# Loading V in 16 KB rows and reordering P by a permuting matmul and a DVE transpose, in a one-core decode kernel

## The chip, the cores and the metric

The kernel runs on one core of a Trainium2 chip. The metric is the device time of one execution in microseconds (us), lower is better. The kernel before takes 418.68 us (median of 4 runs, 418.47 to 418.81). PE is the matmul engine, PEld its weight loads, DVE the vector engine, ACT the scalar engine, POOL the GpSimd engine, and SP issues the DMAs.

## The reference

One token goes through an attention layer with a long cache, beside a small MLP. Cut to what matters here:

```python
# A_x [1,1,1024], k_cache and v_cache [1, 4, 65536, 128] bf16, wq [1024, 4096], wo [4096, 1024]
q = (xn @ wq) -> 32 heads of 128; 8 query heads share one of 4 cache heads
scores = einsum("bhqd,bhkd->bhqk", q, k) * 128 ** -0.5
p = softmax(scores); o = einsum("bhqk,bhkd->bhqd", p, v)
out = x + xn + ...  # o @ wo, and an MLP of w1, w2 [1024, 1024], w3 [1024, 3584], w4 [3584, 1024] on xn
```

K and V are 67.1 MB each, of about 170 MB in all. Each byte is read once and used for 8 query heads, so the kernel is mostly a matter of reading memory: its DMA queue fills 97.8% of the span of the 16 engines (page below).

## The kernel before

It works through 32 blocks (4 cache heads with 8 blocks of 8192 cached positions each). A block brings 2 MB of K and 2 MB of V. The parts that the change and the argument touch (cuts are marked with `# ...`):

```python
NK, NV = 3, 4          # buffers for K and V
KA, VA = 3, 3          # K and V are asked for three blocks ahead

def issue_k(n):        # partition p holds rows 64p..64p+63: one run of 16 KB
    # ...
    e.dma_start(out=Kn[:, s, :, :].rearrange("p c d -> p (c d)"),
                in_=kv_src(A_k_cache, n).rearrange("(p c) d -> p (c d)", p=P))
def issue_v(n):        # four groups of 16 rows a partition: four runs of 4 KB
    # ...
    e.dma_start(out=Vn[:, s, :, :, :].rearrange("p a t d -> p a (t d)"),
                in_=kv_src(A_v_cache, n).rearrange("(a i t) d -> i a (t d)", a=4, i=P))

def Ttr(n, idx):       # DVE: transposes a quarter of K in 32x32 squares, Kn -> X
    # ...
def EXP(n):            # ACT: p = exp(scale * S + running minimum), written at a stride of 8 bytes
    e.activation(p_sb[:, m, :].rearrange("p (cl p0 ch) -> p cl ch p0", cl=4, p0=32),
                 S_ps[:, :].rearrange("p (cl ch p0) -> p cl ch p0", cl=4, ch=4), ACTF.Exp, # ...
def PTr(n):            # PE: four 128x128 transposes of p
    for c2 in range(4): e.transpose(out=PT_ps[:, c2*P:(c2+1)*P], in_=p_sb[:, m, c2*P:(c2+1)*P], identity=ident_bf[:])
def PTevac(n):         # ACT: PSUM -> SBUF, reordered
    e.activation(pT_sb[:, m, :, :, :].rearrange("p r c g -> p c r g"), PT_ps[:, 0:512].rearrange(# ...
def PV(n):             # PE: 16 matmuls of 128x32 by 128x512
    # ...

for n in range(NBLK):
    issue_k(n + KA); issue_v(n + VA); run_pending(n, "dma")   # weights and output rows
    QK(n)
    Ttr(n + 1, [0])
    stats1(n); MB(n); stats2(n); EXP(n)
    Ttr(n + 1, [1, 2, 3])
    PTr(n); PTevac(n); PV(n); FLASH(n)
    # ...
# after the last block: combine the head, ten output rows (wo), seven chunks of w4, output
```

All DMAs are issued by SP in program order, on one queue (30304 of the 30330 packets on the page below). K of block n+3 waits until the transposes of block n have freed its buffer.

Of the kernel before, what the change touches and what calls it, by code (L numbers as in the profile page):

```python
# [6 lines left out]
BF = mybir.dt.bfloat16  # L7
# [124 lines left out]
def bass_parallel_sum__gqa_block_cached__mixer_s_mlp__decode_kernel(  # L132
# [11 lines left out]
    out: bass.AP,  # L144
    dbg=None,
):
    P = 128
# [17 lines left out]
    with ExitStack() as es:  # L165
# [3 lines left out]
        def sb(name, shape, dt):  # L169
            return E(nc.sbuf_tensor(name, shape, dt))  # L170
# [41 lines left out]
        X = sb("X", [P, 2, 8192], BF)  # L212
        Vn = sb("Vn", [P, NV, 4, 16, P], BF)
        tmpO = sb("tmpO", [P, 2, 513], F32)
        p_sb = sb("p_sb", [P, 2, 512], BF)
        pT_sb = sb("pT_sb", [P, 2, 16, 4, G], BF)
        mrow = sb("mrow", [P, 2], F32)
# [23 lines left out]
        S_ps = ps("S_ps", [P, 512], F32)  # L241
        PTB_ps = ps("PTB_ps", [P, 512], F32)
        PT_ps = PTB_ps[:, 0:256].bitcast(BF)
        MB_ps = PTB_ps[:, 256:272]
        OT_ps = ps("OT_ps", [P, 512], F32)
# [36 lines left out]
        def mk_slots():  # L282
            sl = {}
            sl["ws"] = [_Slot(WS[:, i, :], b_WS[i], _DmaChan(sem("d_ws%d" % i))) for i in range(NWS)]
            sl["x"] = [_Slot(X[:, i // 2, 4096 * (i % 2):4096 * (i % 2) + 4096], b_X[i // 2][2 * (i % 2):2 * (i % 2) + 2], _DmaChan(sem("d_x%d" % i)))
                       for i in range(4)]
            sl["k"] = [[_Slot(Kn[:, s, 32 * i:32 * i + 32, :].rearrange("p c k -> p (c k)"), [b_Kn[s][i]], _DmaChan(sem("d_kh%d_%d" % (s, i))))
                        for i in range(2)] for s in range(NK)]
            sl["v"] = [[_Slot(Vn[:, s, 2 * i:2 * i + 2, :, :].rearrange("p a t d -> p (a t d)"), [b_Vn[s][i]], _DmaChan(sem("d_vh%d_%d" % (s, i))))
                        for i in range(2)] for s in range(NV)]  # L290
            return sl
# [4 lines left out]
        for t_, val in ((ident_bf, 0.0), (ident_f, 0.0), (ones_f, 1.0), (sel16, 1.0), (selGT_bf, 1.0), (selTT, 1.0),  # L296
                        (neghalf, -0.5), (permWE, 1.0), (maskA, 1.0), (g_bf, 0.0)):
            evs.append(q_pool.op(lambda e, t_=t_, val=val: e.memset(t_[:], val)))
# [13 lines left out]
                                            compare_op=ALU.is_equal, fill=0.0, base=0, channel_multiplier=1))  # L312
        q_pool.op(lambda e: e.affine_select(out=permWE[:], in_=permWE[:], pattern=[[-64, 2], [-1, 2], [0, 4], [-2, 32]],
                                            compare_op=ALU.is_equal, fill=0.0, base=0, channel_multiplier=1))
        ev = q_pool.op(lambda e: e.affine_select(out=maskA[:], in_=maskA[:], pattern=[[-32, 4], [0, 8]],
# [109 lines left out]
        def issue_v(n):  # L425
            if n >= NBLK:
                return
            s = n % NV
            _dma(q_sp, ch_v[s], lambda e, s=s, n=n: e.dma_start(out=Vn[:, s, :, :, :].rearrange("p a t d -> p a (t d)"),  # L429
                                                                in_=kv_src(A_v_cache, n).rearrange("(a i t) d -> i a (t d)", a=4, i=P)),  # L430
                 writes=b_Vn[s])
# [20 lines left out]
        def QK(n):  # L452
            h = n // NB
            xs = n % 2
            fns = []
            for we in range(4):
                w_hi, e_ = divmod(we, 2)
                for c_mid in range(4):
                    mv = bass.AP(X[:].tensor, xs * 8192 + 4 * c_mid * 128 + w_hi * 64 + e_, [[xstep, P], [128, 4], [2048, 4], [2, 32]])
                    fns.append(lambda e, we=we, c_mid=c_mid, mv=mv, h=h: e.matmul(  # L460
                        S_ps[32 * c_mid:32 * c_mid + 32, :], Yall[:, h, we, :, :].rearrange("p a g -> p (a g)"), mv,
                        start=(we == 0), stop=(we == 3), tile_position=(0, 32 * c_mid)))
            _grp(q_pe, fns, reads=b_X[xs] + [b_Y], writes=[b_S])
# [7 lines left out]
        def MB(n):  # L471
            m = n % 2
            _op(q_pe, lambda e, m=m: e.matmul(MB_ps, Lmat[:, :], Rm[:, m, :], start=True, stop=True),  # L473
                reads=[b_R[m], b_const], writes=[b_MB, b_PT])

        def stats2(n):
            _op(q_dve, lambda e, n=n: e.tensor_reduce(out=Bst[:, n:n + 1], in_=MB_ps, axis=AX.X, op=ALU.min),  # L477
                reads=[b_MB, b_PT], writes=[b_Bcol[n]])

        def EXP(n):  # L480
# [5 lines left out]
            else:  # L486
                ko = (nb - 1) % 2
                _op(q_dve, lambda e, n=n, ko=ko, kn=kn: e.tensor_tensor(out=brun[:, kn:kn + 1], in0=brun[:, ko:ko + 1], in1=Bst[:, n:n + 1], op=ALU.min),  # L488
                    reads=[b_brun[ko], b_Bcol[n]], writes=[b_brun[kn]])
            _op(q_act, lambda e, n=n, m=m, kn=kn: e.activation(p_sb[:, m, :].rearrange("p (cl p0 ch) -> p cl ch p0", cl=4, p0=32),  # L490
                                                               S_ps[:, :].rearrange("p (cl ch p0) -> p cl ch p0", cl=4, ch=4),
                                                               ACTF.Exp, bias=brun[:, kn:kn + 1], scale=SCALE, accum_out=tmpO[:, m, 512:513]),
                reads=[b_S, b_brun[kn]], writes=[b_p[m], b_tmpO[m]])
            if nb > 0:
# [3 lines left out]
                _op(q_act, lambda e, m=m: e.activation(ff[:, m, 0:1], dd[:, m, 0:1], ACTF.Exp), reads=[b_dd[m]], writes=[b_ff[m]])  # L498

        def PTr(n):  # L500
            m = n % 2
            fns = []
            for c2 in range(4):
                fns.append(lambda e, c2=c2, m=m: e.transpose(out=PT_ps[:, c2 * P:(c2 + 1) * P], in_=p_sb[:, m, c2 * P:(c2 + 1) * P], identity=ident_bf[:]))  # L504
            _grp(q_pe, fns, reads=[b_p[m], b_const], writes=[b_PT, b_MB])

        def PTevac(n):
            m = n % 2
            _op(q_act, lambda e, m=m: e.activation(pT_sb[:, m, :, :, :].rearrange("p r c g -> p c r g"),  # L509
                                                   PT_ps[:, 0:512].rearrange("p (c r g) -> p c r g", c=4, r=16), ACTF.Copy),  # L510
                reads=[b_PT, b_MB], writes=[b_pT[m]])

        def PV(n):
            m = n % 2
            vs = n % NV
            fns = []
            for r in range(16):
                q4 = r % 4
                fns.append(lambda e, r=r, q4=q4, m=m, vs=vs: e.matmul(OT_ps[32 * q4:32 * q4 + 32, :], pT_sb[:, m, r, :, :].rearrange("p c g -> p (c g)"),  # L519
                                                                     Vn[:, vs, r % 4, 4 * (r // 4):4 * (r // 4) + 4, :].rearrange("p t d -> p (t d)"),  # L520
                                                                     start=(r < 4), stop=(r >= 12), tile_position=(0, 32 * q4)))
            _grp(q_pe, fns, reads=[b_pT[m]] + b_Vn[vs], writes=[b_OT])
# [166 lines left out]
        for n in range(NBLK):  # L689
# [10 lines left out]
            EXP(n)  # L700
            Ttr(n + 1, [1, 2, 3])
            run_pending(n, "b")
            PTr(n)
            PTevac(n)
            PV(n)
            FLASH(n)
# [19 lines left out]
        _op(q_dve, lambda e: e.tensor_copy(orow[:, :], M0_ps[0:KT_D, 300:300 + P]), reads=[b_M0], writes=[b_orow])  # L726
        if dbg:
            taps = dict(xn=xn[:, :], qT_bf=qT_bf[:, :], Bst=Bst[:, :], Lst=Lst[:, :], O_acc=O_acc[:, :], maskT=maskT[:, :, :].rearrange("p t g -> p (t g)"),
                        OTh_bf=OTh_bf[:, :, :].rearrange("p h g -> p (h g)"), acc=acc[:, :], fin=fin[:, :], p_sb=p_sb[:, :, :].rearrange("p m k -> p (m k)"),
                        pT_sb=pT_sb[:, :, :, :, :].rearrange("p m r c g -> p (m r c g)"), hsT=x1[:, :], h1g=h1g_bf[:, :], gh=gh_bf[:, :],  # L730
                        Yall=Yall[:, :, :, :, :].rearrange("p h w a g -> p (h w a g)"), X=X[:, 0, :], Lmat=Lmat[:, :], sel16=sel16[:, :], selG=selG_f[:, :])
            ch_dbg = _DmaChan(sem("d_dbg"))
            for qq in (q_pe, q_dve, q_act):
                q_pool.wait((qq.sem, qq.cnt))
            for name, dap in dbg.items():
                src = taps[name]
                _dma(q_pool, ch_dbg, lambda e, dap=dap, src=src: e.dma_start(out=dap, in_=src))
                q_pool.wait((ch_dbg.sem, 16 * ch_dbg.n))
        ev_out = _dma(q_sp, ch_out, lambda e: e.dma_start(out=out[0, 0, :].rearrange("(kt p) -> kt p", p=P), in_=orow[:, :]), reads=[b_orow])
# [35 lines left out]
```

## Time and profile before

| | before |
|---|---|
| time, median | 418.68 us |
| span of the profile | 416.8 us |
| hardware DMA queue, share of 16 engines' span | 97.8% |
| busiest compute engine | DVE, 49% |
| K of block 31 taken up, and from there to the end | 380.76 us, 36.0 us |

A packet is one contiguous piece that a DMA engine moves (the trace before holds 16384 packets of 4 KB, as many as V has rows of 4 KB); the profile keeps a record of when each was open. From the page of the kernel before: the DMA busy tenths and the rate in 40 equal slices of the span, the packet count, and the line of the hardware queue (packets, MB, share of the 16 engines' span).

```profile
DMA  7999999999999999999999999999999999999980
GB/s 282 426 420 418 425 424 431 424 425 433 428 425 426 425 426 422 422 417 422 426 431 424 426 424 425 416 426 425 426 425 423 425 424 423 427 417 414 424 366 2
DMA packets 30330, 170.24 MB, mean 408 GB/s; under 512 B 2272, under 2 KB 2272, under 8 KB 23776
...
q1 hardware_dynamic: 30304, 169.88, 97.8%
```

The digits are 9 from the second slice to the 38th, and the rate hardly moves: no slice between shows idle DMA engines. The next fence is the view of windows for the stretch from 50 to 350 us; the columns are named in its first line.

```profile
core 0: us, PE busy (x) PEld busy (x) DVE busy (x) ACT busy (x) POOL busy (x), PEclk, DMA share, GB/s
50.00:350.00 300.00, 140.90 (x1498) 60.76 (x1491) 161.89 (x272) 69.27 (x132) 45.98 (x52) 0.54 1.02 425
```

The costliest groups that the change touches (line, engine, operation, output and input, count | busy us, mean ns | idle time before them and what ended it):

```profile
L448 DVE STREAM_TRANSPOSE X<-Kn 128x1024 f32<-128x1024 f32 x128 | 151.3, 1221 | 131.4 <-DMA Kn<-in_A_k_cache_dram 131.3
L490 ACT ACTIVATE p_sb<-S_ps,brun 128x512 bf16<-128x512 f32 x32 | 44.6, 1395 | 179.2 <-DVE brun L488 156.7
...
L504 PE MATMUL PTB_ps<-ident_bf,p_sb 128*128 128x128 bf16 x128 | 19.2, 305 | 58.0 <-ACT ff L498 54.8
...
L509 ACT ACTIVATE pT_sb<-PTB_ps 128x512 bf16<-128x512 bf16 x32 | 19.1, 597 | 22.3 <-PE PTB_ps L504 22.3
```

DVE waits 131.3 us for K over the kernel, so the compute side has slack in nearly every block. The end is different. These are the DVE instructions of the timeline (start, length, instruction, idle time before it and its releaser) from the last K on:

```profile
380.76 1.25 DVE L448 STREAM_TRANSPOSE X<-Kn 128x1024 f32<-128x1024 f32 x1 [5.54 <-DMA Kn<-in_A_k_cache_dram]
...
383.29 0.16 DVE L488 TENSOR_TENSOR brun<-brun,Bst 128x1 f32<-128x1 f32 x1
...
383.56 3.49 DVE L448 STREAM_TRANSPOSE X<-Kn 128x1024 f32<-128x1024 f32 x3
390.37 0.69 DVE L467 TENSOR_REDUCE mrow<-S_ps 128x1 f32<-128x512 f32 x1 [3.31 <-PE S_ps L460]
```

At 380.76 us DVE takes up K of block 31. From there on there is a chain of compute: the rest of block 30, block 31, the combination of the head, the output rows and w4. The score maximum of block 31, at 390.37 us, is one of its steps, and the span ends at 416.8. So the time is the landing of the last K plus about 36 us.

### The profile page before, as it was taken

Reading aid. Unit: us, or ns where it says so; the run is one execution under the profiler, and the core shown is the slowest. Engines: PE = TensorE matmul, PEld = TensorE weight load, DVE = VectorE, ACT = ScalarE, POOL = GpSimd, SP = SyncE. Lnnn points to the kernel's source line nnn. Section 1 sums busy time; section 2 is a strip of 40 time slices with the busy share of each in tenths; the row PEclk is TensorE's granted clock in tenths of the full one; section 3 lists DMA queues with packets and bytes.
Section 4 is the critical chain, followed back from the end, with each engine's and each line's share of the span. In section 5 each row is a group of like instructions: output and inputs, shape, how many; then the busy total and the mean of one; then the engine's idle time right before and its main releaser. Section 6 shows DMA issues by size and latency. Waiting matters only on the chain.

```text
span 416.8 us, 5862 instructions
## 1 busy us (share of the span) xinstructions
PE 192.5 (46%) x2333; PEld 92.2 (22%) x2333; DVE 202.8 (49%) x369; ACT 84.7 (20%) x159; POOL 60.8 (15%) x86
## 2 busy tenths in 40 slices
PE   1532444434047646424464553345457543333566
PEld 1420111111015312101123221112224111111256
DVE  2037665625466476543345555344556655554200
ACT  0000322312122042221222221122222222121300
POOL 4000011111011121111110111111110111111210
PEclk9999955565565565555655555555555566556555
DMA  7999999999999999999999999999999999999980
GB/s 282 426 420 418 425 424 431 424 425 433 428 425 426 425 426 422 422 417 422 426 431 424 426 424 425 416 426 425 426 425 423 425 424 423 427 417 414 424 366 2
DMA packets 30330, 170.24 MB, mean 408 GB/s; under 512 B 2272, under 2 KB 2272, under 8 KB 23776
## 3 DMA queue, kind: packets, MB, share of 16 engines
q1 hardware_dynamic: 30304, 169.88, 97.8%
q8 instruction: 18, 0.29, 0.3%
q14 instruction: 8, 0.07, 0.0%
HBM read 169.87 MB, written 0.00 MB: 408 GB/s over the span
## 4 chain that ended last, share of the span: by engine, by line
DMA 43%; SPq 36%; PE 7%; DVE 6%; issue 4%; ACT 2%; POOL 0%; POOLq 0%; ACTq 0%; DVEq 0%
DMA Kn<-in_A_k_cache_dram 43%; SPq L435 22%; SPq L429 6%; SPq L422 4%; DVE X L448 3%; PE OT_ps L519 2%; ACT p_sb L490 2%; PE H_ps L388 2%; DVE mrow L467 1%; SPq L673 1%; SPq L342 1%; PE OA_ps L558 1%; PE M_ps L546 1%; PE PTB_ps L504 1%; SPq L579 1%
## 5 line engine op out<-in xcount | busy, mean ns | idle before, releaser
L448 DVE STREAM_TRANSPOSE X<-Kn 128x1024 f32<-128x1024 f32 x128 | 151.3, 1221 | 131.4 <-DMA Kn<-in_A_k_cache_dram 131.3
L490 ACT ACTIVATE p_sb<-S_ps,brun 128x512 bf16<-128x512 f32 x32 | 44.6, 1395 | 179.2 <-DVE brun L488 156.7
L519 PE MATMUL OT_ps<-Vn,pT_sb 128*32 128x512 bf16 x512 | 60.8, 627 | 22.0 <-ACT pT_sb L509 22.0
L460 PE MATMUL S_ps<-X,Yall 128*32 128x512 bf16 x512 | 59.1, 607 | 6.9 <-DVE X L448 6.9
L473 PE MATMUL PTB_ps<-Rm,Lmat 128*128 128x16 bf16 x32 | 6.2, 194 | 107.1 <-DVE Rm L468 107.1
L504 PE MATMUL PTB_ps<-ident_bf,p_sb 128*128 128x128 bf16 x128 | 19.2, 305 | 58.0 <-ACT ff L498 54.8
L533 POOL TENSOR_TENSOR O_acc<-O_acc,tmpO 128x513 f32<-128x513 f32 x28 | 32.8, 1172 | 88.5 <-ACT tmpO L527 88.5
L531 POOL TENSOR_SCALAR O_acc<-O_acc,ff 128x513 f32<-128x513 f32 x28 | 19.5, 698 | 169.1 <-ACT ff L498 169.1
L473 PEld LDWEIGHTS PTB_ps<-Rm,Lmat 128*128 128x128 bf16 x32 | 3.3, 104 | 131.7 <-DVE Rm L468 131.7
L527 ACT ACTIVATE tmpO<-OT_ps 128x512 f32<-128x512 f32 x32 | 19.1, 598 | 64.0 <-PE OT_ps L519 64.0
L519 PEld LDWEIGHTS OT_ps<-Vn,pT_sb 128*32 128x32 bf16 x512 | 14.9, 128 | 47.3 <-ACT pT_sb L509 30.4
L504 PEld LDWEIGHTS PTB_ps<-ident_bf,p_sb 128*128 128x128 bf16 x128 | 10.9, 129 | 60.6 <-ACT ff L498 57.3
L467 DVE TENSOR_REDUCE mrow<-S_ps 128x1 f32<-128x512 f32 x32 | 21.0, 657 | 5.7 <-PE S_ps L460 5.5
L509 ACT ACTIVATE pT_sb<-PTB_ps 128x512 bf16<-128x512 bf16 x32 | 19.1, 597 | 22.3 <-PE PTB_ps L504 22.3
L460 PEld LDWEIGHTS S_ps<-X,Yall 128*32 128x32 bf16 x512 | 15.9, 130 | 28.8 <-issue 21.5
L558 PEld LDWEIGHTS OA_ps<-OTh_bf,wo_sb 128*128 128x128 bf16 x176 | 6.4, 105 | 18.4 <-issue 18.4
L490 ACT ACT_TABLE_LOAD x1 | 1.3, 1283 | 43.3 <-DVE brun L485 43.3
L477 DVE TENSOR_REDUCE Bst<-PTB_ps 128x1 f32<-128x16 f32 x32 | 5.6, 175 | 8.4 <-PE PTB_ps L473 8.4
L529 POOL COPY O_acc<-tmpO 128x513 f32<-128x513 f32 x4 | 2.5, 614 | 48.4 <-ACT tmpO L527 48.4
L388 PE MATMUL H_ps<-xn_bf,WS 128*128 128x1 bf16 x224 | 8.6, 172 | 0.0
L490 ACT ACTIVATION_READ_ACCUMULATOR p_sb<-S_ps,brun 128x1 f32 x32 | 8.3, 259 | 0.0
L558 PE MATMUL OA_ps<-OTh_bf,wo_sb 128*128 128x1 bf16 x176 | 8.2, 168 | 0.0
(107 smaller groups left out, 123.2 us busy)
## 6 DMA issues: line engine op xcount, KB each, us to landing
Kn<-in_A_k_cache_dram SPq DMA_DIRECT2D x32, 2048.0 KB, 23.1
Vn<-in_A_v_cache_dram SPq DMA_DIRECT2D x32, 2048.0 KB, 26.3
WS<-in_B_w_dram SPq DMA_DIRECT2D x8, 896.0 KB, 19.2
wo_sb<-in_A_wo_dram SPq DMA_DIRECT2D x22, 256.0 KB, 25.2
WS<-in_B_w_dram SPq DMA_DIRECT2D x5, 1024.0 KB, 23.5
WS<-in_A_wq_dram SPq DMA_DIRECT2D x4, 1024.0 KB, 8.2
X<-in_A_wq_dram SPq DMA_DIRECT2D x4, 1024.0 KB, 17.0
Kn<-in_B_w_dram SPq DMA_DIRECT2D x4, 1024.0 KB, 15.9
```

The source lines that it names most:

```text
L429: _dma(q_sp, ch_v[s], lambda e, s=s, n=n: e.dma_start(out=Vn[:, s, :, :, :].rearrange("p a t d -> p a (t d)"), in_=kv_src(A_v_cache, n).re ...
L435: _dma(q_sp, ch_wo[ws_], lambda e, h=h, g=g, ws_=ws_: e.dma_start(out=wo_sb[:, ws_, :], in_=A_wo[(h * G + g) * DH:(h * G + g + 1) * DH, :] ...
L448: _op(q_dve, lambda e, ix=ix, ks=ks, xs=xs: e.transpose(out=X32[:, xs, 1024 * ix:1024 * (ix + 1)], in_=Kn32[:, ks, 16 * ix:16 * (ix + 1), ...
L460: fns.append(lambda e, we=we, c_mid=c_mid, mv=mv, h=h: e.matmul(S_ps[32 * c_mid:32 * c_mid + 32, :], Yall[:, h, we, :, :].rearrange("p a g ...
L467: _op(q_dve, lambda e, m=m: e.reduce_max(mrow[:, m:m + 1], S_ps[:, :], axis=AX.X), reads=[b_S], writes=[b_mrow[m]])
L490: _op(q_act, lambda e, n=n, m=m, kn=kn: e.activation(p_sb[:, m, :].rearrange("p (cl p0 ch) -> p cl ch p0", cl=4, p0=32), S_ps[:, :].rearra ...
L504: fns.append(lambda e, c2=c2, m=m: e.transpose(out=PT_ps[:, c2 * P:(c2 + 1) * P], in_=p_sb[:, m, c2 * P:(c2 + 1) * P], identity=ident_bf[:]))
L509: _op(q_act, lambda e, m=m: e.activation(pT_sb[:, m, :, :, :].rearrange("p r c g -> p c r g"), PT_ps[:, 0:512].rearrange("p (c r g) -> p c ...
L519: fns.append(lambda e, r=r, q4=q4, m=m, vs=vs: e.matmul(OT_ps[32 * q4:32 * q4 + 32, :], pT_sb[:, m, r, :, :].rearrange("p c g -> p (c g)") ...
L527: _op(q_act, lambda e, m=m: e.activation(tmpO[:, m, 0:512], OT_ps[:, :], ACTF.Copy), reads=[b_OT], writes=[b_tmpO[m]], partial=True)
L531: _op(q_pool, lambda e, m=m: e.tensor_scalar(out=O_acc[:, :], in0=O_acc[:, :], scalar1=ff[:, m, 0:1], scalar2=0.0, op0=ALU.mult, op1=ALU.add),
L533: _op(q_pool, lambda e, m=m: e.tensor_tensor(out=O_acc[:, :], in0=O_acc[:, :], in1=tmpO[:, m, :], op=ALU.add), reads=[b_tmpO[m]], writes=[ ...
```

## The change

Its intent: load V in the same layout as K, one run of 16 KB a partition instead of four of 4 KB, so that the DMA moves fewer and larger pieces. The order of the rows in a partition then changes, and P, the softmax weights of a block (`p` in the code), has to come out in the matching order. This is done by one matmul with a permutation matrix and one DVE transpose from PSUM (the program's indices take it in squares of 32x32), in place of four PE transposes and an ACT eviction; EXP can then write contiguously. The second half of the K transposes moves behind the new DVE transpose.

```diff
-        in_=kv_src(A_v_cache, n).rearrange("(a i t) d -> i a (t d)", a=4, i=P)
+        in_=kv_src(A_v_cache, n).rearrange("(p c) d -> p (c d)", p=P)
@@ QK
-    mv = bass.AP(X[:].tensor, xs * 8192 + 4 * c_mid * 128 + w_hi * 64 + e_, [[xstep, P], [128, 4], [2048, 4], [2, 32]])
+    mv = bass.AP(X[:].tensor, xs * 8192 + c_mid * 128 + w_hi * 64 + e_, [[xstep, P], [512, 16], [2, 32]])
@@ EXP
-    e.activation(p_sb[:, m, :].rearrange("p (cl p0 ch) -> p cl ch p0", ...), S_ps[:, :].rearrange(...), ACTF.Exp, ...)
+    e.activation(p_sb[:, m, :], S_ps[:, :], ACTF.Exp, ...)
@@ PTr
-    for c2 in range(4): e.transpose(out=PT_ps[:, c2*P:(c2+1)*P], in_=p_sb[:, m, c2*P:(c2+1)*P], identity=ident_bf[:])
+    e.matmul(PT_ps[:, :], permR[:, :], p_sb[:, m, :], start=True, stop=True)
@@ PTevac
-    q_act: e.activation(pT_sb[...], PT_ps[:, 0:512]..., ACTF.Copy)
+    q_dve: e.transpose(out=pT_f[:, m, :], in_=PT_ps[:, :])
@@ PV
-    weights pT_sb[:, m, r, :, :], moving Vn[:, vs, r % 4, 4 * (r // 4):4 * (r // 4) + 4, :]
+    weights pT_bf[:, m, q, :, 1] (upper halves of the f32 words), moving Vn[:, vs, 4 * q:4 * q + 4, :]
@@ the loop
-            Ttr(n + 1, [1, 2, 3])
+            Ttr(n + 1, [1])
             run_pending(n, "b")
             PTr(n)
             PTevac(n)
+            Ttr(n + 1, [2, 3])
             PV(n)
(cut: buffers, a PSUM bank of its own for MB, the constant permR, and debug code that never ran)
```

More of the change, by code (lines that the diff above doesn't have):

```diff
@@ L144, in bass_parallel_sum__gqa_block_cached__mixer_s_mlp__decode_kernel @@
     out: bass.AP,
-    dbg=None,
 ):
@@ L212, in bass_parallel_sum__gqa_block_cached__mixer_s_mlp__decode_kernel @@
         X = sb("X", [P, 2, 8192], BF)
-        Vn = sb("Vn", [P, NV, 4, 16, P], BF)
+        Vn = sb("Vn", [P, NV, 64, P], BF)
         tmpO = sb("tmpO", [P, 2, 513], F32)
         p_sb = sb("p_sb", [P, 2, 512], BF)
-        pT_sb = sb("pT_sb", [P, 2, 16, 4, G], BF)
+        pT_f = sb("pT_f", [P, 2, 512], F32)
+        permR = sb("permR", [P, P], BF)
         mrow = sb("mrow", [P, 2], F32)
@@ L241, in bass_parallel_sum__gqa_block_cached__mixer_s_mlp__decode_kernel @@
         S_ps = ps("S_ps", [P, 512], F32)
-        PTB_ps = ps("PTB_ps", [P, 512], F32)
-        PT_ps = PTB_ps[:, 0:256].bitcast(BF)
-        MB_ps = PTB_ps[:, 256:272]
+        PT_ps = ps("PT_ps", [P, 512], F32)
+        MBB_ps = ps("MBB_ps", [P, 512], F32)
+        MB_ps = MBB_ps[:, 0:16]
         OT_ps = ps("OT_ps", [P, 512], F32)
@@ L288, in mk_slots @@
                         for i in range(2)] for s in range(NK)]
-            sl["v"] = [[_Slot(Vn[:, s, 2 * i:2 * i + 2, :, :].rearrange("p a t d -> p (a t d)"), [b_Vn[s][i]], _DmaChan(sem("d_vh%d_%d" % (s, i))))
+            sl["v"] = [[_Slot(Vn[:, s, 32 * i:32 * i + 32, :].rearrange("p c d -> p (c d)"), [b_Vn[s][i]], _DmaChan(sem("d_vh%d_%d" % (s, i))))
                         for i in range(2)] for s in range(NV)]
@@ L296, in bass_parallel_sum__gqa_block_cached__mixer_s_mlp__decode_kernel @@
         for t_, val in ((ident_bf, 0.0), (ident_f, 0.0), (ones_f, 1.0), (sel16, 1.0), (selGT_bf, 1.0), (selTT, 1.0),
-                        (neghalf, -0.5), (permWE, 1.0), (maskA, 1.0), (g_bf, 0.0)):
+                        (neghalf, -0.5), (permWE, 1.0), (permR, 1.0), (maskA, 1.0), (g_bf, 0.0)):
             evs.append(q_pool.op(lambda e, t_=t_, val=val: e.memset(t_[:], val)))
@@ L313, in bass_parallel_sum__gqa_block_cached__mixer_s_mlp__decode_kernel @@
         q_pool.op(lambda e: e.affine_select(out=permWE[:], in_=permWE[:], pattern=[[-64, 2], [-1, 2], [0, 4], [-2, 32]],
+                                            compare_op=ALU.is_equal, fill=0.0, base=0, channel_multiplier=1))
+        q_pool.op(lambda e: e.affine_select(out=permR[:], in_=permR[:], pattern=[[-8, 4], [-32, 4], [-1, 8]],
                                             compare_op=ALU.is_equal, fill=0.0, base=0, channel_multiplier=1))
@@ L428, in issue_v @@
             s = n % NV
-            _dma(q_sp, ch_v[s], lambda e, s=s, n=n: e.dma_start(out=Vn[:, s, :, :, :].rearrange("p a t d -> p a (t d)"),
-                                                                in_=kv_src(A_v_cache, n).rearrange("(a i t) d -> i a (t d)", a=4, i=P)),
+            _dma(q_sp, ch_v[s], lambda e, s=s, n=n: e.dma_start(out=Vn[:, s, :, :].rearrange("p c d -> p (c d)"), in_=kv_src(A_v_cache, n).rearrange("(p c) d -> p (c d)", p=P)),
                  writes=b_Vn[s])
@@ L473, in MB @@
             _op(q_pe, lambda e, m=m: e.matmul(MB_ps, Lmat[:, :], Rm[:, m, :], start=True, stop=True),
-                reads=[b_R[m], b_const], writes=[b_MB, b_PT])
+                reads=[b_R[m], b_const], writes=[b_MB])
         def stats2(n):
             _op(q_dve, lambda e, n=n: e.tensor_reduce(out=Bst[:, n:n + 1], in_=MB_ps, axis=AX.X, op=ALU.min),
-                reads=[b_MB, b_PT], writes=[b_Bcol[n]])
+                reads=[b_MB], writes=[b_Bcol[n]])
         def EXP(n):
@@ L489, in EXP @@
                     reads=[b_brun[ko], b_Bcol[n]], writes=[b_brun[kn]])
-            _op(q_act, lambda e, n=n, m=m, kn=kn: e.activation(p_sb[:, m, :].rearrange("p (cl p0 ch) -> p cl ch p0", cl=4, p0=32),
-                                                               S_ps[:, :].rearrange("p (cl ch p0) -> p cl ch p0", cl=4, ch=4),
-                                                               ACTF.Exp, bias=brun[:, kn:kn + 1], scale=SCALE, accum_out=tmpO[:, m, 512:513]),
+            _op(q_act, lambda e, n=n, m=m, kn=kn: e.activation(p_sb[:, m, :], S_ps[:, :], ACTF.Exp, bias=brun[:, kn:kn + 1], scale=SCALE, accum_out=tmpO[:, m, 512:513]),
                 reads=[b_S, b_brun[kn]], writes=[b_p[m], b_tmpO[m]])
@@ L498, in EXP @@
                 _op(q_act, lambda e, m=m: e.activation(ff[:, m, 0:1], dd[:, m, 0:1], ACTF.Exp), reads=[b_dd[m]], writes=[b_ff[m]])
+        pT_bf = pT_f[:].bitcast(BF).rearrange("p m (q r two) -> p m q r two", q=16, two=2)
         def PTr(n):
             m = n % 2
-            fns = []
-            for c2 in range(4):
-                fns.append(lambda e, c2=c2, m=m: e.transpose(out=PT_ps[:, c2 * P:(c2 + 1) * P], in_=p_sb[:, m, c2 * P:(c2 + 1) * P], identity=ident_bf[:]))
-            _grp(q_pe, fns, reads=[b_p[m], b_const], writes=[b_PT, b_MB])
+            _op(q_pe, lambda e, m=m: e.matmul(PT_ps[:, :], permR[:, :], p_sb[:, m, :], start=True, stop=True),
+                reads=[b_p[m], b_const], writes=[b_PT])
         def PTevac(n):
             m = n % 2
-            _op(q_act, lambda e, m=m: e.activation(pT_sb[:, m, :, :, :].rearrange("p r c g -> p c r g"),
-                                                   PT_ps[:, 0:512].rearrange("p (c r g) -> p c r g", c=4, r=16), ACTF.Copy),
-                reads=[b_PT, b_MB], writes=[b_pT[m]])
+            _op(q_dve, lambda e, m=m: e.transpose(out=pT_f[:, m, :], in_=PT_ps[:, :]), reads=[b_PT], writes=[b_pT[m]])
         def PV(n):
@@ L516, in PV @@
             fns = []
-            for r in range(16):
-                q4 = r % 4
-                fns.append(lambda e, r=r, q4=q4, m=m, vs=vs: e.matmul(OT_ps[32 * q4:32 * q4 + 32, :], pT_sb[:, m, r, :, :].rearrange("p c g -> p (c g)"),
-                                                                     Vn[:, vs, r % 4, 4 * (r // 4):4 * (r // 4) + 4, :].rearrange("p t d -> p (t d)"),
-                                                                     start=(r < 4), stop=(r >= 12), tile_position=(0, 32 * q4)))
+            for q in range(16):
+                q4 = q % 4
+                fns.append(lambda e, q=q, q4=q4, m=m, vs=vs: e.matmul(OT_ps[32 * q4:32 * q4 + 32, :], pT_bf[:, m, q, :, 1],
+                                                                     Vn[:, vs, 4 * q:4 * q + 4, :].rearrange("p t d -> p (t d)"),
+                                                                     start=(q < 4), stop=(q >= 12), tile_position=(0, 32 * q4)))
             _grp(q_pe, fns, reads=[b_pT[m]] + b_Vn[vs], writes=[b_OT])
@@ L726, in bass_parallel_sum__gqa_block_cached__mixer_s_mlp__decode_kernel @@
         _op(q_dve, lambda e: e.tensor_copy(orow[:, :], M0_ps[0:KT_D, 300:300 + P]), reads=[b_M0], writes=[b_orow])
-        if dbg:
-            taps = dict(xn=xn[:, :], qT_bf=qT_bf[:, :], Bst=Bst[:, :], Lst=Lst[:, :], O_acc=O_acc[:, :], maskT=maskT[:, :, :].rearrange("p t g -> p (t g)"),
-                        OTh_bf=OTh_bf[:, :, :].rearrange("p h g -> p (h g)"), acc=acc[:, :], fin=fin[:, :], p_sb=p_sb[:, :, :].rearrange("p m k -> p (m k)"),
-                        pT_sb=pT_sb[:, :, :, :, :].rearrange("p m r c g -> p (m r c g)"), hsT=x1[:, :], h1g=h1g_bf[:, :], gh=gh_bf[:, :],
-                        Yall=Yall[:, :, :, :, :].rearrange("p h w a g -> p (h w a g)"), X=X[:, 0, :], Lmat=Lmat[:, :], sel16=sel16[:, :], selG=selG_f[:, :])
-            ch_dbg = _DmaChan(sem("d_dbg"))
-            for qq in (q_pe, q_dve, q_act):
-                q_pool.wait((qq.sem, qq.cnt))
-            for name, dap in dbg.items():
-                src = taps[name]
-                _dma(q_pool, ch_dbg, lambda e, dap=dap, src=src: e.dma_start(out=dap, in_=src))
-                q_pool.wait((ch_dbg.sem, 16 * ch_dbg.n))
         ev_out = _dma(q_sp, ch_out, lambda e: e.dma_start(out=out[0, 0, :].rearrange("(kt p) -> kt p", p=P), in_=orow[:, :]), reads=[b_orow])
```

## The prediction

> **What bounds the kernel now.** The DMA engines: the queue table gives the hardware queue 97.8% of 16 engines' span, the slices show 414 to 433 GB/s nearly throughout; no compute engine is over 49% busy. In the chain of waits 43% is the landing of K, and most of the 36% on the issuing queue is issues[...] (7 to 9 us for a 256 KB row). DVE's K transposes wait 131.3 us for K, about 4.7 a block. Only the last 36 us (K of block 31 is taken up at 380.76, the span ends at 416.8) are a compute chain; the last bytes land near 405.5 and do not bind.
>
> **The change, costed.**
> 1. V goes from 16384 packets of 4 KB to 4096 of 16 KB, same bytes. In the trace's packet records a 4 KB packet takes 159.4 ns of an engine, a 16 KB one (K) 613.4; all sizes fit about 8.7 ns + 37.6 ns per KB. V costs 16384 x 159.4 / 16 = 163.3 us of span now, 4096 x 613.4 / 16 = 157.0 after: 6.25 saved.[...]
> 2. EXP writes contiguously instead of at an 8-byte stride: 1395 ns now; the plain 128x512 eviction takes 598, so I estimate 600 to 750.
> 3. Four transposes (0.61 us) become one 128x512 matmul[...].
> 4. The ACT eviction (597 ns) becomes a DVE transpose, estimated 0.65 us from half of the 1221 ns of a 128x1024 one. DVE gains about 21 us busy, ACT loses about 40.
> 5. The last two K transposes of the next block now stand behind it: X is ready, and K's buffer free, about 1.1 us later. But they overlap PV: from the running minimum to the next QK I estimate 4.8 us against 5.2 (timeline, block 30). A block's compute cycle, 8 to 9 us, stays under its 9.8 us or more of DMA. K lands 23 us after issue, so about two blocks are queued; releasing 1 us later opens no gap.
> 6. One memset and one select more on POOL at the start, hidden behind the wq load.
>
> **On the critical path.** Item 1 almost whole: 31 of 32 V loads precede K of block 31, which lands 31/32 x 6.25 = 6.05 us earlier. In the closing compute chain items 2 to 5 give about 0.2 us in block 30, 0.8 in block 31. Elsewhere compute savings vanish in the wait for K. Sum: 7 us.
>
> **Prediction:** 418.6 - 7 = 411.7 us, 8 in 10 between 410.4 and 414.0. Faster by over 2% 0.08, within 2% 0.89, slower 0.03.
>
> **What would show each step.** About 18000 packets instead of 30330, no V packets of 4 KB, 16 KB packets near 613 ns, about 428 GB/s mid-stretch, DMA over 97%. DVE's wait for K above 3.5 us a block. K of block 31 taken up near 374.7 us, about 35 us to the end. EXP and the new DVE transpose each near 0.65 us.
>
> **What would make it wrong.** 16 KB packets slow down when both K and V use them: less is saved, or nothing. K released so late that the queue empties: DMA share falls, the issuing queue waits for DVE. The transpose from PSUM or PV's stride-2 weight loads cost far more, pushing a block over its DMA time. EXP stays at 1.4 us: costs 0.8.

The sum came to 7 us: 6.05 of item 1 and about 1.0 of items 2 to 5.

## The result

| | before | after |
|---|---|---|
| time, median | 418.68 us (4 runs) | 413.90 us (4 runs, 413.73 to 413.96) |
| ratio | | 0.9889 (95%: 0.9875 to 0.9903) |
| K of block 31 taken up | 380.76 us | 376.81 us |
| from there to the end of the span | 36.0 us | 35.2 us |

A ratio is the mean time of one kernel's fast runs over that of the other's of the same rounds, so it is not quite the ratio of the medians.

The gain is about 4.8 us where 7 were predicted. It splits at the landing of the last K: 3.95 us before it (6.05 predicted), 0.8 us after it (1.0 predicted). The page after, the same lines:

```profile
DMA  7999999999999999999999999999999999999990
GB/s 280 426 435 430 433 429 431 424 437 425 431 433 428 428 429 429 427 421 436 430 426 429 431 425 427 426 433 428 425 431 428 431 429 426 425 422 421 423 387 13
DMA packets 18043, 170.25 MB, mean 413 GB/s; under 512 B 2272, under 2 KB 2272, under 8 KB 7392
...
q1 hardware_dynamic: 18016, 169.88, 97.5%
```

The packets fell from 30330 to 18043, as forecast, and the engines are as full as before. The windows view of the same stretch:

```profile
core 0: us, PE busy (x) PEld busy (x) DVE busy (x) ACT busy (x) POOL busy (x), PEclk, DMA share, GB/s
50.00:350.00 300.00, 146.38 (x1452) 55.30 (x1448) 182.99 (x300) 39.85 (x107) 46.72 (x52) 0.60 1.01 429
```

The DMA share fell from 1.02 to 1.01 while the rate rose from 425 to 429 GB/s. The groups:

```profile
L449 DVE STREAM_TRANSPOSE X<-Kn 128x1024 f32<-128x1024 f32 x128 | 153.6, 1221 | 104.2 <-DMA Kn<-in_A_k_cache_dram 104.1
...
L491 ACT ACTIVATE p_sb<-S_ps,brun 128x512 bf16<-128x512 f32 x32 | 22.0, 687 | 188.9 <-DVE brun L489 168.9
...
L503 PE MATMUL PT_ps<-p_sb,permR 128*128 128x512 bf16 x32 | 19.2, 600 | 40.0 <-ACT p_sb L491 40.0
...
L508 DVE STREAM_TRANSPOSE pT_f<-PT_ps 128x512 f32<-128x512 f32 x32 | 22.9, 717 | 9.8 <-PE PT_ps L503 9.8
```

EXP went from 1395 to 687 ns. The DVE transpose takes 717 ns, and the single matmul 600. The DVE instructions of the end:

```profile
376.81 1.25 DVE L449 STREAM_TRANSPOSE X<-Kn 128x1024 f32<-128x1024 f32 x1 [4.50 <-DMA Kn<-in_A_k_cache_dram]
...
379.34 0.16 DVE L489 TENSOR_TENSOR brun<-brun,Bst 128x1 f32<-128x1 f32 x1
...
381.06 0.72 DVE L508 STREAM_TRANSPOSE pT_f<-PT_ps 128x512 f32<-128x512 f32 x1 [0.22 <-PE PT_ps L503]
381.70 2.33 DVE L449 STREAM_TRANSPOSE X<-Kn 128x1024 f32<-128x1024 f32 x2
386.08 0.69 DVE L468 TENSOR_REDUCE mrow<-S_ps 128x1 f32<-128x512 f32 x1 [2.05 <-PE S_ps L461]
```

The two K transposes at 381.70 stand behind the transpose of P at 381.06, as ordered. The score maximum of block 31 starts at 386.08, which is 6.74 us after the running minimum (379.34); before, it was 390.37 - 383.29 = 7.08 us.

### The profile page after: what moved, and what is told of

The parts are those of the page before. It is cut to its first block, busy times and chain, and to the rows that moved or that the text cites. A ratio compares the mean times of both kernels' runs of the same rounds, so it can differ in the third digit from the quotient of the medians.

```text
span 412.0 us, 5690 instructions
## 1 busy us (share of the span) xinstructions
PE 194.8 (47%) x2237; PEld 84.4 (20%) x2237; DVE 226.0 (55%) x401; ACT 48.4 (12%) x127; POOL 61.4 (15%) x88
## 2 busy tenths in 40 slices
DMA packets 18043, 170.25 MB, mean 413 GB/s; under 512 B 2272, under 2 KB 2272, under 8 KB 7392
## 3 DMA queue, kind: packets, MB, share of 16 engines
q1 hardware_dynamic: 18016, 169.88, 97.5%
## 4 chain that ended last, share of the span: by engine, by line
DMA 56%; DVE 18%; PE 11%; SPq 7%; issue 4%; ACT 3%; POOL 1%; POOLq 0%; ACTq 0%; DVEq 0%
DMA Kn<-in_A_k_cache_dram 51%; DVE X L449 10%; DMA X<-in_A_wq_dram 5%; SPq L670 4%; ACT p_sb L491 2%; DVE pT_f L508 2%; DVE mrow L468 2%; PE PT_ps L503 2%; PE S_ps L461 2%; PE H_ps L390 2%; PE M_ps L543 1%; PE OT_ps L516 1%; SPq L436 1%; PE OA_ps L555 1%; SPq L344 1%
## 5 line engine op out<-in xcount | busy, mean ns | idle before, releaser
L449 DVE STREAM_TRANSPOSE X<-Kn 128x1024 f32<-128x1024 f32 x128 | 153.6, 1221 | 104.2 <-DMA Kn<-in_A_k_cache_dram 104.1
L516 PE MATMUL OT_ps<-Vn,pT_f 128*32 128x512 bf16 x512 | 60.7, 627 | 25.9 <-DVE pT_f L508 25.9
L474 PE MATMUL MBB_ps<-Rm,Lmat 128*128 128x16 bf16 x32 | 6.2, 195 | 109.8 <-DVE Rm L469 109.8
L491 ACT ACTIVATE p_sb<-S_ps,brun 128x512 bf16<-128x512 f32 x32 | 22.0, 687 | 188.9 <-DVE brun L489 168.9
L503 PE MATMUL PT_ps<-p_sb,permR 128*128 128x512 bf16 x32 | 19.2, 600 | 40.0 <-ACT p_sb L491 40.0
L508 DVE STREAM_TRANSPOSE pT_f<-PT_ps 128x512 f32<-128x512 f32 x32 | 22.9, 717 | 9.8 <-PE PT_ps L503 9.8
L516 PEld LDWEIGHTS OT_ps<-Vn,pT_f 128*32 128x32 bf16 x512 | 14.7, 129 | 58.9 <-DVE pT_f L508 41.9
L503 PEld LDWEIGHTS PT_ps<-p_sb,permR 128*128 128x128 bf16 x32 | 3.9, 122 | 42.6 <-ACT p_sb L491 42.6
L478 DVE TENSOR_REDUCE Bst<-MBB_ps 128x1 f32<-128x16 f32 x32 | 5.6, 175 | 8.4 <-PE MBB_ps L474 8.4
L390 PEld LDWEIGHTS H_ps<-xn_bf,WS 128*128 128x128 bf16 x224 | 8.1, 117 | 0.0
L543 PE MATMUL M_ps<-cb_W,O_acc 128*128 128x8 f32 x32 | 7.5, 364 | 1.0 <-DVE cb_W L537 1.0
## 6 DMA issues: line engine op xcount, KB each, us to landing
Kn<-in_A_k_cache_dram SPq DMA_DIRECT2D x32, 2048.0 KB, 26.3
```

The source lines that it names most:

```text
L390: e.matmul(ps_tile[:, col0 + ncx:col0 + ncx + 1], lhs_fn(kk, ncx), rhs_fn(kt + kk), start=st, stop=(kt + kk == nkt - 1), skip_group_check= ...
L449: _op(q_dve, lambda e, ix=ix, ks=ks, xs=xs: e.transpose(out=X32[:, xs, 1024 * ix:1024 * (ix + 1)], in_=Kn32[:, ks, 16 * ix:16 * (ix + 1), ...
L491: _op(q_act, lambda e, n=n, m=m, kn=kn: e.activation(p_sb[:, m, :], S_ps[:, :], ACTF.Exp, bias=brun[:, kn:kn + 1], scale=SCALE, accum_out= ...
L503: _op(q_pe, lambda e, m=m: e.matmul(PT_ps[:, :], permR[:, :], p_sb[:, m, :], start=True, stop=True), reads=[b_p[m], b_const], writes=[b_PT])
L508: _op(q_dve, lambda e, m=m: e.transpose(out=pT_f[:, m, :], in_=PT_ps[:, :]), reads=[b_PT], writes=[b_pT[m]])
L516: fns.append(lambda e, q=q, q4=q4, m=m, vs=vs: e.matmul(OT_ps[32 * q4:32 * q4 + 32, :], pT_bf[:, m, q, :, 1], Vn[:, vs, 4 * q:4 * q + 4, : ...
```

## The experiments

The theory that I formed from the two traces (A): the records of packets on one engine overlap, so their lengths overstate what a packet costs, and more so for small packets. Rival B: packets cost what their records say, 6 us were saved, and the reordered compute gives 2 of them back by freeing K's buffers later. Twelve kernels were run, the control among them, each with 4 or 5 timed runs. "K31" is the time at which K of block 31 is taken up, "rest" is from there to the end of the span. The kernel before had medians of 418.77, 418.55 and 418.46 us on the three chips used.

| run | what it is | median us | ratio to before | K31 | rest |
|---|---|---|---|---|---|
| b_v16k | before, V in 16 KB rows | 414.81 | 0.9904 | 377.25 | 36.0 |
| a_v4k | after, V in 4 KB pieces 32 B apart | 418.96 | 1.0004 | 382.09 | 35.2 |
| a_v8k | after, V in 8 KB pieces 32 B apart | 415.39 | 0.9919 | 378.36 | 35.3 |
| a_v2k | after, V in 2 KB pieces 32 B apart | 427.03 | 1.0194 | 389.68 | 35.4 |
| a_v4k_old | after, the V load of before | 417.96 | 0.9985 | 380.68 | 35.3 |
| a_ttr_first | after, K transposes first | 415.44 | 0.9929 | 376.80 | 36.7 |
| a_va2 | after, V two blocks ahead | 410.83 | 0.9803 | 371.94 | 37.2 |
| b_va2 | before, V two blocks ahead | 415.91 | 0.9931 | 375.48 | 38.4 |
| a_v4k_pad256 | after, V in 4 KB pieces 256 B apart | 417.48 | 0.9976 | 380.43 | 35.2 |
| a_v2k_old | after, V in 2 KB rows, eight groups | 423.05 | 1.0106 | 386.04 | 35.2 |
| a_va2_wolate | a_va2, output rows later | 409.71 | 0.9790 | 368.15 | 40.1 |
| after_again | after, control | 413.93 | 0.9891 | 376.86 | 35.3 |

### b_v16k: the V load alone

```diff
 (before)
-    in_=kv_src(A_v_cache, n).rearrange("(a i t) d -> i a (t d)", a=4, i=P)
+    in_=kv_src(A_v_cache, n).rearrange("(p c) d -> p (c d)", p=P)
```

> The kernel before with only the V load changed to 16 KB rows; P keeps its old order, so the result is wrong on purpose. Theory A (packet records of one engine overlap, a packet costs its engine about 5.3 ns: 3.95 us x 16 / (31 x 384 packets)): K of block 31 is taken up 3.9 to 4.0 us earlier than in the kernel before, tail unchanged at 36.0 us, about 414.7 us. Theory B (a packet costs 8.7 ns as its records say, and the reordered compute of the changed kernel gives 2 us of it back by freeing K late): 6.05 us earlier, about 412.6 us.

Measured 414.81 us against 418.77. The windows line from 50 to 350 us, and then the take-up of the last K in the timeline:

```profile
50.00:350.00 300.00, 143.83 (x1525) 61.76 (x1518) 163.82 (x273) 70.23 (x134) 46.85 (x52) 0.56 1.01 429
```

```profile
377.25 1.25 DVE L448 STREAM_TRANSPOSE X<-Kn 128x1024 f32<-128x1024 f32 x1 [5.43 <-DMA Kn<-in_A_k_cache_dram]
```

K31 came 3.5 us earlier, and the time fell by 4.0 us (A: about 414.7 us, B: 412.6), with the compute as it was and no reordering at all. Theory A holds and B falls: the missing 2 us were never saved, so nothing gave them back. The profiled execution was the slowest of its four (415.20 us; the others 414.71 to 414.88), and its stream of K began late: the second K, the first that DVE has to wait for, was taken up 0.30 us later than in the kernel before. The two lines, before and then this run:

```profile
39.95 1.25 DVE L448 STREAM_TRANSPOSE X<-Kn 128x1024 f32<-128x1024 f32 x1 [0.40 <-DMA Kn<-in_A_k_cache_dram]
40.25 1.25 DVE L448 STREAM_TRANSPOSE X<-Kn 128x1024 f32<-128x1024 f32 x1 [0.24 <-DMA Kn<-in_A_k_cache_dram]
```

From the second K to K31 this run gains 3.8 us on the kernel before; the traces of after and after_again gain 3.9 and 3.8 over the same stretch. The V load alone gives all of the gain at K31. (By construction P no longer meets its own V rows; the correctness test passed all the same, so it would not catch a wrong order here.)

### a_v4k, a_v8k, a_v2k: packet sizes, result right

```diff
 (after; NCH = 2, 4, 8 pieces of CH = 8192 / NCH elements, PADE = 16)
-        Vn = sb("Vn", [P, NV, 64, P], BF)
+        Vn = sb("Vn", [P, NV, NCH, CH + PADE], BF)
-    out=Vn[:, s, :, :]..., in_=kv_src(A_v_cache, n).rearrange("(p c) d -> p (c d)", p=P)
+    out=Vn[:, s, :, 0:CH], in_=kv_src(A_v_cache, n).rearrange("(p a t) d -> p a (t d)", p=P, a=NCH)
```

> The changed kernel with V in 4 KB packets again (same rows in the same partitions; the pieces of one partition lie 32 bytes apart in SBUF[...]); result right. Theory A: about 413.9 + 4.0 = 417.9 us, so that the compute part of the change is worth 0.8 us alone. Theory B: the compute part alone costs about 1 to 2 us net, so about 419.5 to 420 us, slower than the kernel before. If it is not packet size but the order in which the memory is read, this stays at 413.9 us.

> V in 8 KB packets, 4096 packets more than the changed kernel, result right. Theory A at 5.3 ns: +1.3 us, about 415.2. Theory B at 8.7 ns: +2.2 us, about 416.1.

> V in 2 KB packets, 28672 packets more than the changed kernel, result right. Theory A at 5.3 ns: 31/32 x 28672 x 5.3 / 16 = +9.2 us, about 423.1. Theory B at 8.7 ns: +15.1 us, about 429.0. In the trace theory A also wants the mean number of packet records open at once above 16 by more than in any other run.

Measured 418.96, 415.39 and 427.03 us. The 8 KB run agrees with A. The 4 KB run lies between A (417.9) and B (419.5 to 420), and the 2 KB run lies nearer B (429.0) than A (423.1), so this set alone did not decide. Two things had been changed at once, the size of the packets and the place of the pieces in SBUF, and the next runs took them apart.

### a_v4k_old: the other corner of a two by two table

```diff
 (after)
-    out=Vn[:, s, :, :]..., in_=kv_src(A_v_cache, n).rearrange("(p c) d -> p (c d)", p=P)
+    out=Vn[:, s, :, :].rearrange("p (a t) d -> p a (t d)", a=4), in_=kv_src(A_v_cache, n).rearrange("(a i t) d -> i a (t d)", a=4, i=P)
```

> The changed kernel with exactly the V load of the kernel before (4 KB rows, four row groups); P no longer matches its V rows, so the result is wrong on purpose (the check may not notice: the weights are nearly uniform). With the two kernels and the earlier run that changed V alone this closes a two by two table. If the parts add up: the closing chain 0.85 us shorter, K of block 31 taken up as in the kernel before near 380.8 us, about 417.8 us; then the slower 418.96 of the run with pieces 32 bytes apart was its own access pattern. If the reordered compute costs DMA time: 418.9 us again.

Measured 417.96 us against 418.55. The windows line and the take-up of the last K:

```profile
50.00:350.00 300.00, 133.38 (x1398) 54.06 (x1408) 180.34 (x298) 39.21 (x106) 46.20 (x51) 0.53 1.02 425
```

```profile
380.68 1.25 DVE L449 STREAM_TRANSPOSE X<-Kn 128x1024 f32<-128x1024 f32 x1 [4.71 <-DMA Kn<-in_A_k_cache_dram]
```

K31 at 380.68 is that of the kernel before (380.76), so the reordered compute costs the DMA nothing. The rest is 35.3 us instead of 36.0. The parts add up, to within what the runs can tell: V alone takes 4.0 us off (418.77 to 414.81), compute alone 0.6 (418.55 to 417.96), both together 4.8.

### a_v4k_pad256: where the pieces lie

```diff
 (a_v4k)
-        PADE = 16       # elements of 2 bytes between pieces
+        PADE = 128
```

> As the earlier run with V in 4 KB pieces, 418.96 us, but the pieces of one partition lie 256 bytes apart in SBUF instead of 32; result right. The memory is read in the same order. If the 1.0 us over the run with the old V load (417.96) comes from where the pieces lie in SBUF, this run falls to about 418.0 us; if from the order in which the rows are read, it stays at 419.0.

Measured 417.48 us: with 256 bytes between the pieces the excess of a_v4k is gone. The windows lines of a_v4k, and then of this run:

```profile
50.00:350.00 300.00, 133.45 (x1402) 54.01 (x1411) 179.42 (x297) 38.73 (x104) 45.54 (x51) 0.56 1.02 423
```

```profile
50.00:350.00 300.00, 133.29 (x1398) 54.10 (x1408) 180.70 (x299) 39.26 (x106) 46.32 (x51) 0.54 1.02 425
```

The rate goes from 423 back to 425 GB/s, that of the kernel before, at the same size of packet and the same order of reading. So the 1 us was the 32-byte spacing of the pieces in SBUF, not packet size and not the order in memory; why that spacing costs time was not tried. This run also settles a rival to packet size itself. It reads the rows in the order of the kernel after, yet in 4 KB packets, and its last K comes when that of the kernel before does (380.76):

```profile
380.43 1.25 DVE L451 STREAM_TRANSPOSE X<-Kn 128x1024 f32<-128x1024 f32 x1 [4.61 <-DMA Kn<-in_A_k_cache_dram]
```

The change gained by its larger packets, not by the order in which it reads.

### a_v2k_old: more packets, no spacing

```diff
 (after)
+    out=Vn[:, s, :, :].rearrange("p (a t) d -> p a (t d)", a=8), in_=kv_src(A_v_cache, n).rearrange("(a i t) d -> i a (t d)", a=8, i=P)
```

> The changed kernel with V in 2 KB rows in the row-group order of the kernel before (eight groups); result wrong on purpose. Stretches of the trace of before in which only V or only K move show 422.0 and 431.9 GB/s, so a 4 KB packet costs its engine 155.3 ns and a 16 KB one 606.9, which is 4.8 ns a packet. With 28672 packets more than the changed kernel: 31/32 x 28672 x 4.8 / 16 = +8.3 us, about 422.2 us. If the packets really cost 8.7 ns: +15.1 us, 429.0. If 2 KB packets have a cost of their own beyond that, as the run with pieces 32 bytes apart showed (+13.1 us), near 427.

Measured 423.05 us (expected 422.2, rival 429.0), 9.1 us over the control. The windows line:

```profile
50.00:350.00 300.00, 133.52 (x1405) 54.12 (x1413) 176.60 (x290) 38.34 (x103) 45.80 (x51) 0.57 1.03 419
```

The DMA share rose to 1.03 as the rate fell to 419: the share counts overlap, not work.

K and V come in turn, so every trace has stretches in which only one size of packet is open. I took stretches of half a microsecond between about 50 and 340 us in which over 99.9% of the open packet records are of one size, and worked out the medians from the records:

| packet | mean record, ns | records open at once | rate, GB/s | time of one engine per packet, 16 x size / rate, ns | from |
|---|---|---|---|---|---|
| 2 KB | 84.4 | 16.80 | 409.5 | 80.0 | a_v2k_old |
| 4 KB | 159.5 | 16.38 | 422.0 | 155.3 | before |
| 8 KB | 310.5 | 16.17 | 428.2 | 306.1 | a_v8k |
| 16 KB | 612.8 | 16.10 | 431.8 | 607.1 | after |

The engine's time is fitted by 4.7 ns + 37.65 ns per KB to within 0.2 ns. (The 8 KB pieces of a_v8k lie 32 bytes apart; their rate shows nothing of it.) The records give 8.7 ns + 37.8 ns per KB. The difference, 4 to 6 ns a packet, is overlap with other packets. With these times V costs 16384 x 155.3 / 16 = 159.0 us in 4 KB packets and 4096 x 607.1 / 16 = 155.4 in 16 KB packets: 3.6 us saved, and 31/32 of it, 3.5, before K31. Measured at K31 were 3.5 (b_v16k, after its late start) and 3.9 (after, twice). The lines for 4 KB and 16 KB were both in the trace of the kernel before, so this could have been predicted.

### a_ttr_first: the order of the K transposes

```diff
 (after)
-            Ttr(n + 1, [1])
+            Ttr(n + 1, [1, 2, 3])
             PTr(n); PTevac(n)
-            Ttr(n + 1, [2, 3])
```

> The changed kernel with all three K transposes ahead of the P transpose on DVE, as in the kernel before; result right. K buffers are freed 0.7 us earlier, P is ready later. If DMA bounds the middle, K of block 31 stays at 376.8 us and only the closing chain changes: the P transpose of block 30 starts about 3.7 us after the minimum instead of 1.7, so QK of block 31 starts about 6.8 us after it instead of 4.8: about +1.5 to 2 us, 415.6 us. If the later release of K cost DMA time, K of block 31 would be earlier instead.

Measured 415.44 us against 413.9. The DVE instructions at the end:

```profile
376.80 1.25 DVE L449 STREAM_TRANSPOSE X<-Kn 128x1024 f32<-128x1024 f32 x1 [4.84 <-DMA Kn<-in_A_k_cache_dram]
...
379.60 3.49 DVE L449 STREAM_TRANSPOSE X<-Kn 128x1024 f32<-128x1024 f32 x3
383.01 0.67 DVE L508 STREAM_TRANSPOSE pT_f<-PT_ps 128x512 f32<-128x512 f32 x1
387.83 0.69 DVE L468 TENSOR_REDUCE mrow<-S_ps 128x1 f32<-128x512 f32 x1 [4.14 <-PE S_ps L461]
```

K31 is at 376.80, unchanged to a hundredth, though K's buffers are freed earlier. The transpose of P starts at 383.01 instead of 381.06, and the maximum of block 31 at 387.83 instead of 386.08. So the new order is worth 1.5 us, all of it in the closing chain, and neither order touches the DMA. This is the second finding against B.

### a_va2 and b_va2: K further ahead of V

```diff
-    KA, VA = 3, 3
+    KA, VA = 3, 2
```

> The changed kernel with V asked for two blocks ahead instead of three, so that K of a block goes ahead of V of the block before in the queue; result right. If the end is a compute chain that starts at the landing of K of block 31 and V of block 31 has about a block of slack, that K lands 4.9 us earlier (one V load), the chain stays near 35.2 us, about 409.0 us; bytes and packets do not change. If the chain is bound by V or by the last weights instead, 413 to 414 us.

> The kernel before with that one change of the V distance; result right. Same reading: 4.9 us earlier with the 36.0 us chain, about 413.8 us, as much as the whole studied change. If V's arrival binds, less.

Measured 410.83 and 415.91 us. For a_va2, the take-up of the last K in the timeline:

```profile
371.94 1.25 DVE L449 STREAM_TRANSPOSE X<-Kn 128x1024 f32<-128x1024 f32 x1 [4.44 <-DMA Kn<-in_A_k_cache_dram]
```

K31 came 4.9 us earlier, just as the reading of the chain says, with the same bytes and packets. But only 3.1 us of it arrived, and in b_va2 2.6. The chain after K31 had grown to 37.2 and 38.4 us. PE instructions of a_va2 in the timeline:

```profile
402.34 0.40 PE L390 MATMUL H_ps<-gh_bf,Vn 128*128 128x1 bf16 x10
404.58 1.56 PE L390 MATMUL H_ps<-gh_bf,Vn 128*128 128x1 bf16 x42 [1.83 <-issue]
```

PE stopped for 1.83 us in the middle of a group of w4 matmuls that share one wait, so it waited for no data there ("issue" means that the profile shows nothing that it waited for). b_va2 has such a stop of 2.39 us. In both traces a 16 KB packet of the instruction queue landed 1.2 to 1.3 us before PE went on, while the last weights were still being loaded. What PE waited for no run tested; it stays open. The five times of a_va2 fall into two groups, 409.82 and 409.86, and 410.83 to 410.87; the profiled execution is of the slower group, so the stop may not come in every execution.

### a_va2_wolate: the last output rows behind the last K

```diff
 (a_va2)
-    at(min(t_ws_free + i // 2, t0), "dma", lambda i=i: issue_wo_tail_row(i))
+    at(t0, "dma", lambda i=i: issue_wo_tail_row(i))
```

> The run with V two blocks ahead (410.8 us), and the last ten output rows asked for after K of block 31 too; result right. K of block 31 lands about 6 us earlier still, near 366 us, and the compute chain would end near 401; but the last weights still land near 403.4 us, and PE needs 1.1 us for the last chunk and about 2.7 us to the end, so DMA binds the end: about 409.0 us. If PE again stalls for 2 us among the last weight chunks[...], near 410.8 again.

Measured 409.71 us, the fastest kernel of this study: 0.979 of the kernel before (0.9776 to 0.9803), 2.1% faster, with a right result; since the interval reaches over 0.98, faster by 2% is not settled. It improves on a_va2 by 1.1 us at the medians; they ran on different chips, and the intervals of their ratios touch (a_va2: 0.9789 to 0.9816), and two of the five runs of a_va2 were as fast (409.82 and 409.86), so that step is not settled. K31 came 3.8 us earlier than in a_va2, not 6: four of the ten rows had been behind that K already, and six rows of about 0.6 us are 3.7. PE stopped twice:

```profile
393.77 0.46 PE L390 MATMUL H_ps<-gh_bf,Kn 128*128 128x1 bf16 x12
396.92 0.69 PE L390 MATMUL H_ps<-gh_bf,Kn 128*128 128x1 bf16 x20 [2.70 <-issue]
...
401.18 0.40 PE L390 MATMUL H_ps<-gh_bf,Vn 128*128 128x1 bf16 x10
403.69 0.74 PE L390 MATMUL H_ps<-gh_bf,Vn 128*128 128x1 bf16 x22 [2.11 <-issue]
```

Two stops of 2.70 and 2.11 us among the weight chunks, and again PE went on about 1.4 us after the landing of an instruction packet (395.5 and 402.3 us). The trace says more. From the end of one stop to the end of the other PE runs 126 matmuls, 126 weight loads and 4 semaphore instructions, 256 in all, and the stop of a_va2 ends at the same instruction as the second of these. So that stop kept its place in the program while its end moved from 404.58 to 403.69 us. What PE waited for is not shown here either.

### after_again: the control

> The changed kernel itself once more, as a control on this chip: 413.9 us, 0.989 of the kernel before, K of block 31 taken up at 376.8 us.

Measured 413.93 us, ratio 0.9891, K31 at 376.86 us. The result stands on a second chip.

## Why the prediction was right or wrong

- **What bounds the kernel: right.** DMA in the middle, a compute chain from K31 on. K31 moved with V's load (b_v16k), and by one V load when the queue order changed (a_va2).
- **Packets, sizes, shares: right.** 18043 packets for "about 18000", a 97.5% share, 16 KB packets at 613 ns also when K and V both use them, 429 GB/s for "about 428", a wait for K of 104.1 / 27 = 3.9 us a block for "above 3.5".
- **The step that failed: "6.25 saved" of item 1, taken as "6.05 us earlier" for K31.** K31 came 3.95 us earlier. The term was mis-sized because "a 4 KB packet takes 159.4 ns of an engine, a 16 KB one (K) 613.4" is the length of a record, and records on one engine overlap by about 4 ns. Of the "about 8.7 ns" a packet only 4.7 cost time, so 12288 packets fewer save 12288 x 4.7 / 16 = 3.6 us. The 4.7 ns explain 3.5 of the 3.95; 0.4 us is not explained. It is no accident of one trace, since all three traces with 16 KB packets gain 3.8 or 3.9 us from the second K to K31, about 5.3 ns a packet (the 2 KB rows also cost 9.2 us at K31 where 4.7 ns a packet make 8.2).
- **The prediction contradicted itself.** It forecast "about 428 GB/s mid-stretch". From 425, over the 370 us or so before K31, that is 0.7%, 2.6 us, not 6. Forecasting a time and a rate separately and comparing them would have shown the fault.
- **Items 2 to 5 in the closing chain: right in sum.** About 1.0 predicted, 0.8 measured (36.0 to 35.2 us). EXP at 687 ns was inside 600 to 750. The matmul took 600 ns, as long as the four transposes together (0.61 us), and the DVE transpose 717, not 650. The difference of 0.2 us no run took apart.
- **Item 5, K freed later without harm: right.** a_ttr_first frees K earlier and K31 does not move; a_v4k_old frees it later than before and K31 does not move. SP does wait for DVE now (224.4 us in its waits, 43.6 before), but the engines stay full (97.5%); the prediction's reason, about two blocks in the queue, fits (K took 23.1 us from issue to landing in the kernel before, 26.3 after) and was not tested.
- **The time** of 413.9 us is 0.1 us from the upper end of 410.4 to 414.0, and the class, within 2%, was right; the predicted gain of 7 us was half as much again as the measured 4.8.

## What to carry to other kernels

Cost a change of packet size by rates, not by record lengths: find stretches in the trace with one size only and compare bytes per time there (here that gives 3.5 us before K31 and the records gave 6.05, for 3.95 measured). In this profile a DMA share over 1 was the sign that records overlap. Then ask which landing ends the DMA-bound part. In this kernel one number that set which tensor comes first in the queue gave 2.6 to 3.1 us for no work at all, more than half of what the studied change gave.
